# Splitting the second pair's key loads and the first value load in a decode-attention kernel

## The chip, the cores and the metric

The kernel runs on one core of a Trainium2 chip. The metric is the time of one execution on the device in microseconds (us). Engines are called as in the profile: PE is TensorE's matmul side, PEld its weight loads, DVE VectorE, ACT ScalarE, SP the sync engine, which here issues nearly all DMA loads. A ratio of two kernels is the mean time of one's fast runs over the mean of the other's fast runs in the same rounds, so it isn't quite the ratio of the medians that are quoted beside it.

## The reference

One decode step: attention of 16 query heads over a cache of 8192 positions (8 key/value heads of width 256, batch 4), with a small MLP as a gate.

```python
x = A_x                                   # [4, 1, 448] bf16
xn = layernorm(x)
q = (xn @ wq) -> [B, 16, 1, 256]
k, v = repeat(k_cache, 2), repeat(v_cache, 2)   # caches [4, 8, 8192, 256] bf16
p = softmax(einsum("bhqd,bhkd->bhqk", q, k) * 256**-0.5)
s = einsum("bhqk,bhkd->bhqd", p, v) @ wo
return x + s * silu(B(xn))                # B: the gate, on [4, 448] only
```

The two caches are 268 MB, each byte is used once, and all loads together are 279 MB. Everything else is small.

## The kernel before

The 32 key/value heads (8 in each of the 4 batch entries) are worked on in 16 pairs. `kn` holds the keys of one pair (two slots `t` of 4 MiB, 32 KB a partition each), `vb` its values (8 MiB, one buffer). Each of PE's 16 passes transposes the pair's keys through PSUM, makes the scores, and, at the end, multiplies the probabilities of the **pair before** with that pair's values in `vb`. The first pass has no pair before: its value products run on zeros in `pT` and whatever `vb` holds (weights, then), and only afterwards may the first values be loaded into `vb`.

The loads, all from SP, in order:

```python
def load_k(i, t):                       # keys of pair i, slot t
    if i == 0:
        load(kv, src, lo, mid, "dk%d" % t); load(kv, src, mid, hi, "dkh%d" % t)
    elif (i, t) == (1, 1):
        sp.wait_ge(S["v_k"], NVK * (i - 1) + 2)     # first half of slot 1 is free
        load(kv, src, lo, mid, "dk%d" % t)
        sp.wait_ge(S["v_k"], NVK * i)               # second half too
        load(kv, src, mid, hi, "dkh%d" % t)
    else:
        sp.wait_ge(S["v_k"], NVK * (i - 1) + (1, NVK)[t])
        load(kv, src, lo, hi, "dk%d" % t)           # 4 MiB, 32 KB a partition
        ...
def load_v(i):                          # values of pair i
    if i < NPAIR - 1:
        sp.wait_ge(S["v_v"], i + 1)
        load(vv, src, 0, NC2, "dv")                 # 8 MiB, 64 KB a partition
    ...
load_k(0, 0); load_k(0, 1)
load_wo(NLATE, HQ, "dwo")               # early part of the output weights, 2.2 MB
for i in range(1, NPAIR):
    load_k(i, 0); load_k(i, 1); load_v(i - 1)
```

The end of a pass on PE. `PV_PARTS` says how many of the 128 pieces of values are done between which of the last scores:

```python
PV_PARTS = (0, 8, 16, 28, 72, NC2)
for i, f in enumerate(tail):            # last three scores, then two steps of the row maximum
    if t == NS - 1:
        f_pv(vv, PV_PARTS[i], PV_PARTS[i + 1], NC2)   # signals p_pv after the last one
    f()
f_sum()
```

And on DVE, where `v_v` is what releases `vb` to the next load:

```python
f_negb()                                # waits for PE's step after the last value product
f_rz()
take(v, "p_pv")
v.sem_inc(S["v_v"], 1)
v.sem_inc(S["v_pt"], 1)
f_po()
```

## Time and profile before

| | before |
|---|---|
| median time | 656.48 us (655.72 to 656.78, 3 runs) |
| profiled run | 657.7 us, span 656.4 us |
| bytes loaded | 279 MB |
| PE busy / ACT busy / DVE busy | 77% / 40% / 39% |

The first view is the page of the profiled run of the kernel before: its span, then three rows in 40 equal slices of 16.4 us each. PEclk is PE's granted clock in tenths (9 is 90% or more), DMA the busy share of the 16 DMA engines in tenths, GB/s what they moved.

```profile
span 656.4 us, 21990 instructions
...
PEclk9997999899796979969697796969989697998967
DMA  9998999999999999999999999999999999999997
GB/s 378 433 429 348 383 445 449 415 423 439 433 461 413 417 447 447 447 401 429 445 446 417 431 433 433 457 415 419 445 425 467 409 425 445 445 417 425 439 426 297
...
```

DMA is busy in every slice. The fourth and fifth slices (49 to 82 us) with 348 and 383 GB/s stand out. A packet counts in the slice in which it begins, so with packets of up to 64 KB single slices scatter about the true rate, up to 467 GB/s here. Spread over each packet's own duration (worked out from the packed trace, since no view prints it), the rate between 100 and 600 us is 433.7 GB/s; 433.6 is used from here on.

The DMA view of the same kernel: all packets, then for two kinds of load the count, the size of one where it is known, and the median us from issue to landing.

```profile
DMA packets 10641, 279.13 MB, mean 425 GB/s; under 512 B 1028, under 2 KB 3080, under 8 KB 3592
...
kn<-in_A_k_cache_dram SPq DMA_DIRECT2D x29, 4096.0 KB, 26.5
...
vb<-in_A_v_cache_dram SPq DMA_DIRECT2D x15, 29.9
```

A load of 4 MiB takes 9.7 us at 433.6 GB/s, yet a typical one lands 26.5 us after its issue: it stands in a queue behind others. With that backlog an earlier issue in later pairs should buy nothing. PE, in turn, waits for the loads.

So the time of this kernel is: bytes over 433.6 GB/s (643.7 us), plus what follows the last landing (2.9 us), plus every stretch in which the DMA engines run dry: 2.6 us in the first 40 us, 5.3 us between 40 and 72 us, and 1.9 us between 600 us and the last landing. The sum is 656.4 us, the span. Here are the stretches of the first pass, from the view by windows. The columns are the window, its length, the busy us and the number of instructions of each engine, the granted clock, the DMA's busy share, and GB/s:

```profile
core 0: us, PE busy (x) PEld busy (x) DVE busy (x) ACT busy (x) POOL busy (x), PEclk, DMA share, GB/s
52.00:56.00 4.00, 1.89 (x46) 1.72 (x43) 0.82 (x2) 1.39 (x2) 0.00 (x0) 1.00 0.91 377
56.00:60.00 4.00, 4.00 (x69) 2.15 (x70) 1.34 (x2) 0.65 (x1) 0.00 (x0) 0.62 0.93 360
60.00:64.00 4.00, 4.00 (x39) 1.11 (x35) 1.44 (x5) 0.00 (x0) 0.00 (x0) 0.52 0.86 348
64.00:68.00 4.00, 3.38 (x56) 2.51 (x48) 2.00 (x5) 1.61 (x8) 0.00 (x0) 1.00 0.87 295
68.00:72.00 4.00, 3.45 (x83) 3.33 (x83) 1.61 (x3) 3.54 (x6) 0.00 (x0) 1.00 0.60 262
```

Here the DMA falls behind for 20 us. These are most of the 5.3 us of loading that are lost between 40 and 72 us. SP's timeline of the same kernel shows the issues (start us, us to issue):

```profile
38.52 0.33 SPq L252 DMA_DIRECT2D kn<-in_A_k_cache_dram  x1
50.12 0.33 SPq L252 DMA_DIRECT2D kn<-in_A_k_cache_dram  x1
57.02 0.33 SPq L252 DMA_DIRECT2D kn<-in_A_k_cache_dram  x1
66.19 0.33 SPq L252 DMA_DIRECT2D vb<-in_A_v_cache_dram  x1
```

These are the first loads of the second pair's keys for slot 0 (4 MiB) and slot 1 (2 MiB at 50.12, 2 MiB at 57.02), and the first values. The last keys land at 66.1 us, the values are issued at 66.19: nothing is queued in between. What the values waited for stands in DVE's timeline; the releasing instruction is between L524 and L528:

```profile
...
65.41 0.16 DVE L520 COPY negb<-psm 128x4 f32<-128x4 f32 x1 [1.83 <-DVEq L307]
65.72 0.18 DVE L524 RECIPROCAL rz<-psw 128x4 f32<-128x4 f32 x1 [0.15 <-DVEq L307]
66.35 0.69 DVE L528 COPY po<-psv 128x512 f32<-128x512 f32 x1 [0.44 <-DVEq L307]
...
```

PE is late in this pass for a reason of its own. Its timeline has these three idle times that nothing in the profile explains ("issue"; the bracket is the idle time before the row):

```profile
36.94 0.24 PE L650 MATMUL psc<-qc,kT 128*128 128x4 bf16 x4 [0.65 <-issue]
...
46.54 0.35 PE L650 MATMUL psc<-qc,kT 128*128 128x4 bf16 x8 [3.81 <-issue]
...
55.11 0.40 PE L637 MATMUL pst<-ident_b,kn 128*128 128x128 bf16 x4 [2.11 <-issue]
```

They lie exactly 124 matmuls apart. With the weight loads, waits and branches between them these are 256 or 257 recorded PE instructions. The DMA records of the packed trace (again in no view) show a fetch of 16 KB of instructions that was done 1.4 us before each gap ended (packets from 34.6, 44.2 and 52.8 us, 0.92 to 0.97 us each). That PE waited for these fetches is the author's reading; the trace shows only the order in time. A boundary (also "block boundary") is one of these places among PE's instructions, passed when PE does the matmul at which the gap ended here. A fetch's delay is counted from the boundary before: the one at 52.8 us began 6.2 us after PE passed the boundary at 46.5.

### The profile page before, as it was taken

The numbers are of one execution on the slowest core, as the hardware profiler recorded it, in microseconds if no ns is written. First come the engines' busy times: TensorE is split into PE (matmuls) and PEld (weight loads), VectorE is DVE, ScalarE is ACT, GpSimd is POOL, SyncE is SP. The second block draws the span as 40 slices with busy tenths as digits, with TensorE's granted clock in tenths as the row PEclk, the third lists the DMA queues.
The fourth block names the chain that finished last, engine by engine and source line by source line (L and its number), as shares of the span: only waits on it lengthen the run. The fifth ranks groups of instructions, "written<-read, shape, count | busy, mean of one in ns | idle before, by whom it ended". The sixth has DMA issues, their size and how long they took to land. (4 is left out here: it accounts for less than half of the span.)

```text
span 656.4 us, 21990 instructions
## 1 busy us (share of the span) xinstructions
PE 502.7 (77%) x9693; PEld 408.6 (62%) x9693; DVE 257.1 (39%) x507; ACT 263.1 (40%) x360; POOL 3.7 (1%) x18
## 2 busy tenths in 40 slices
PE   2878979686895958679594986958589595867957
PEld 0765869476492947649284583938558293765914
DVE  7433545343351524425252352524335152433511
ACT  3432645254260625426063361615436062543601
POOL 2000000000000000000000000000000000000000
PEclk9997999899796979969697796969989697998967
DMA  9998999999999999999999999999999999999997
GB/s 378 433 429 348 383 445 449 415 423 439 433 461 413 417 447 447 447 401 429 445 446 417 431 433 433 457 415 419 445 425 467 409 425 445 445 417 425 439 426 297
DMA packets 10641, 279.13 MB, mean 425 GB/s; under 512 B 1028, under 2 KB 3080, under 8 KB 3592
## 3 DMA queue, kind: packets, MB, share of 16 engines
q1 hardware_dynamic: 10616, 278.99, 98.9%
q8 instruction: 7, 0.11, 0.1%
q14 instruction: 2, 0.02, 0.0%
q10 hardware_dynamic: 16, 0.01, 0.0%
HBM read 278.99 MB, written 0.00 MB: 425 GB/s over the span
## 5 line engine op out<-in xcount | busy, mean ns | idle before, releaser
L637 PE MATMUL pst<-ident_b,kn 128*128 128x128 bf16 x4096 | 300.4, 221 | 23.7 <-PEq L307 21.6
L341 ACT ACTIVATE kT<-pst 128x1024 bf16<-128x1024 bf16 x224 | 226.0, 1023 | 114.1 <-ACTq L307 113.9
L339 DVE COPY kT<-pst 128x1024 bf16<-128x1024 bf16 x288 | 197.5, 691 | 173.7 <-DVEq L307 173.6
L637 PEld LDWEIGHTS pst<-ident_b,kn 128*128 128x128 bf16 x4096 | 238.1, 98 | 25.4 <-issue 25.4
L650 PE MATMUL psc<-qc,kT 128*128 128x4 bf16 x4096 | 174.1, 165 | 11.6 <-PEq L307 6.7
L682 PE MATMUL psv<-vb,pT 128*8 128x512 bf16 x1024 | 106.4, 515 | 98.8 <-PEq L307 98.8
L650 PEld LDWEIGHTS psc<-qc,kT 128*128 128x128 bf16 x4096 | 153.2, 97 | 41.5 <-issue 40.7
L364 ACT ACTIVATE pT<-psc,negb 64x128 bf16<-64x128 f32 x64 | 28.4, 535 | 247.7 <-ACTq L307 247.4
L682 PEld LDWEIGHTS psv<-vb,pT 128*8 128x8 bf16 x1024 | 25.3, 96 | 133.5 <-issue 124.3
L499 DVE TENSOR_REDUCE rmax<-psc 64x2 f32<-64x256 f32 x32 | 13.5, 422 | 137.6 <-DVEq L307 137.4
L675 PE MATMUL psm<-sel,po 128*128 128x4 f32 x136 | 19.2, 264 | 1.6 <-PEq L307 1.6
L675 PEld LDWEIGHTS psm<-sel,po 128*128 128x128 f32 x136 | 18.1, 204 | 1.7 <-issue 1.7
L364 ACT ACTIVATION_READ_ACCUMULATOR pT<-psc,negb 64x1 f32 x64 | 16.4, 256 | 0.0
L528 DVE COPY po<-psv 128x512 f32<-128x512 f32 x17 | 11.7, 691 | 11.5 <-DVEq L307 11.5
L509 DVE TENSOR_REDUCE gmax<-psm 2x2 f32<-2x128 f32 x16 | 4.5, 279 | 26.8 <-DVEq L307 26.8
L520 DVE COPY negb<-psm 128x4 f32<-128x4 f32 x16 | 2.6, 162 | 25.7 <-DVEq L307 25.7
L663 PEld LDWEIGHTS psm<-diag,ones_f 2*128 2x128 f32 x32 | 4.7, 182 | 7.0 <-issue 7.0
L659 PEld LDWEIGHTS psm<-ident_f,rmax 128*2 128x2 f32 x16 | 1.3, 81 | 12.0 <-issue 12.0
L582 PE MATMUL pst<-ident_b,xn_b 4*128 4x4 bf16 x14 | 0.7, 163 | 10.0 <-DVE xn_b L411 10.0
L582 PEld LDWEIGHTS pst<-ident_b,xn_b 4*128 4x128 bf16 x14 | 0.5, 100 | 10.9 <-issue 9.7
L667 PE MATMUL psw<-rowsum,ones_f 128*128 128x4 f32 x34 | 6.7, 269 | 0.0
L663 PE MATMUL psm<-diag,ones_f 2*128 2x4 f32 x32 | 6.1, 258 | 0.0
(93 smaller groups left out, 84.5 us busy)
## 6 DMA issues: line engine op xcount, KB each, us to landing
kn<-in_A_k_cache_dram SPq DMA_DIRECT2D x29, 4096.0 KB, 26.5
kn<-in_A_k_cache_dram SPq DMA_DIRECT2D x6, 2048.0 KB, 24.3
kn<-in_A_v_cache_dram SPq DMA_DIRECT2D x1, 4096.0 KB, 27.7
vb<-in_A_wq_dram SPq DMA_DIRECT2D x1, 3584.0 KB, 11.4
vb<-in_B_w_dram SPq DMA_DIRECT2D x2, 1568.0 KB, 15.7
wo_sb<-in_A_wo_dram SPq DMA_DIRECT2D x1, 2240.0 KB, 40.4
kn<-in_A_v_cache_dram SPq DMA_DIRECT2D x1, 2048.0 KB, 26.2
kn<-in_A_v_cache_dram SPq DMA_DIRECT2D x1, 1280.0 KB, 24.7
```

The source lines that it names most:

```text
L339: engine.tensor_copy(dst, src).then_inc(S["v_ev"], 1)
L341: engine.activation(dst, src, ACT.Copy).then_inc(S["a_ev"], 1)
L364: ins = act.activation(pT[own, 0:NC2 * NR].rearrange("p (c n) -> p n c", n=NR)[:, n], psc[own, 0:NC2 * NR].rearrange("p (c n) -> p n c", n ...
L499: ins = v.tensor_reduce(rmax[own, :], psc[own, 0:NC2 * NR].rearrange("p (c n) -> p n c", n=NR)[:, t * REP:(t + 1) * REP], AX.X, ALU.max)
L509: v.tensor_reduce(gmax[:, :], psm[0:REP, 0:P].rearrange("p (s k) -> p s k", s=NS), AX.X, ALU.max).then_inc(S["v_s"], 1)
L528: v.tensor_copy(po[:, :], psv[:, 0:CP * DH]).then_inc(S["v_po"], 1)
L637: ins = pe.transpose(dst[:, n * P:(n + 1) * P], kn[:, t, GC * j + kl, half * P:(half + 1) * P], ident_b[:, :])
L650: ins = pe.matmul(psc[:, kk * NR:(kk + 1) * NR], kT[:, j % RING, n * P:(n + 1) * P], qc[:, :, half, :], start=(half == 0), stop=(half == N ...
L663: pe.matmul(psm[:, P:P + NR], ones_f[0:REP, :], diag[:, :], start=True, stop=True).then_inc(S["p_m2"], 1)
L667: pe.matmul(psw[:, 0:NR], ones_f[:, :], rowsum[:, :], start=True, stop=True).then_inc(S["p_s"], 1)
L675: ins = pe.matmul(psm[:, o:o + NR], po[:, i * DH + dh:(i + 1) * DH:NHALF], sel[:, i, 0:NR], start=(i == 0), stop=(i == CP - 1))
L682: ins = pe.matmul(psv[o:o + CP * NR, 0:CP * DH], pT[:, kk * NR:(kk + CP) * NR], src[:, kk:kk + CP, :].rearrange("p c d -> p (c d)"), start ...
```

## The change

Its intent: let the DMA run on where it runs dry, by (1) loading the second pair's keys in pieces of 8 KB a partition, (2) loading the first values in two halves, each released when PE's value products have passed it, and (3) releasing `vb` on DVE before two small operations. The boundary 72 of the value products moves to 64, so that a half ends on it.

```diff
+    NKP = 4
-    PV_PARTS = (0, 8, 16, 28, 72, NC2)
+    PV_PARTS = (0, 8, 16, 28, NCH, NC2)          # NCH = 64
 ...                                              # load_k
+                sp.wait_ge(S["v_k"], NVK * (i - 1) + 1 + t)
+                if i == 1:
+                    for n in range(NKP):
+                        if t == 1 and n == NKP // 2:
+                            sp.wait_ge(S["v_k"], NVK * i)
+                        load(kv, src, lo + n * NCH // NKP, lo + (n + 1) * NCH // NKP, "dk%d" % t)
 ...                                              # load_v
-                if i < NPAIR - 1:
+                if i == 0:
+                    sp.wait_ge(S["p_vh"], 1)
+                    load(vv, src, 0, NCH, "dv")
+                    sp.wait_ge(S["v_v"], 1)
+                    load(vv, src, NCH, NC2, "dv")
+                elif i < NPAIR - 1:
                     sp.wait_ge(S["v_v"], i + 1)
                     load(vv, src, 0, NC2, "dv")
 ...                                              # DVE, end of a pass
+                take(v, "p_pv")
+                v.sem_inc(S["v_v"], 1)
                 f_negb()
                 f_rz()
-                take(v, "p_pv")
-                v.sem_inc(S["v_v"], 1)
                 v.sem_inc(S["v_pt"], 1)
 ...                                              # PE, end of a pass
-                            f_pv(vv, PV_PARTS[i], PV_PARTS[i + 1], NC2)
+                            ins = f_pv(vv, PV_PARTS[i], PV_PARTS[i + 1], NC2)
+                            if PV_PARTS[i + 1] == NCH:
+                                ins.then_inc(S["p_vh"], 1)
+                            if PV_PARTS[i + 1] == NC2:
+                                ins.then_inc(S["p_pv"], 1)
```

The rest of the diff only makes the semaphore counts agree (a slot of keys now counts 64, a pair's values 32) and signals the last pair's products from the place where `f_pv` is called. No arithmetic is added.

More of the change, by code (lines that the diff above doesn't have):

```diff
@@ L198, in bass_recurrent_scan__gqa_block_cached__mixer_s_mlp__decode_kernel @@
         S = {n: es.enter_context(nc.semaphore(n)) for n in (
-            ["dx", "dwq", "dw3", "dw4", "dwo", "dk0", "dk1", "dkh0", "dkh1", "dv", "dout", "pause"]
+            ["dx", "dwq", "dw3", "dw4", "dwo", "dk0", "dk1", "dkh0", "dkh1", "dv", "p_vh", "dout", "pause"]
             + ["dvl%d" % i for i in range(NPIECE)] + ["dwl%d" % i for i in range(len(LATE))]
@@ L261, in load_k @@
                     load(kv, src, mid, hi, "dkh%d" % t)
-                elif (i, t) == (1, 1):
-                    sp.wait_ge(S["v_k"], NVK * (i - 1) + 2)
-                    load(kv, src, lo, mid, "dk%d" % t)
-                    sp.wait_ge(S["v_k"], NVK * i)
-                    load(kv, src, mid, hi, "dkh%d" % t)
-                else:
-                    sp.wait_ge(S["v_k"], NVK * (i - 1) + (1, NVK)[t])
+                    sp.sem_inc(S["dk%d" % t], 16 * (NKP - 1))
+                    return
+                sp.wait_ge(S["v_k"], NVK * (i - 1) + 1 + t)
[4 more added lines that the diff above has]
+                        load(kv, src, lo + n * NCH // NKP, lo + (n + 1) * NCH // NKP, "dk%d" % t)
+                else:
+                    if t == 1:
+                        sp.wait_ge(S["v_k"], NVK * i)
                     load(kv, src, lo, hi, "dk%d" % t)
-                    if t == 1:
-                        sp.sem_inc(S["dkh1"], 16)
+                    sp.sem_inc(S["dk%d" % t], 16 * (NKP - 1))
             def load_v(i):
                 src = pair(A_v_cache, i)
-                if i < NPAIR - 1:
+                if i == 0:
[4 more added lines that the diff above has]
+                elif i < NPAIR - 1:
                     sp.wait_ge(S["v_v"], i + 1)
                     load(vv, src, 0, NC2, "dv")
+                    sp.sem_inc(S["dv"], 16)
                 else:
@@ L449, in prog_dve @@
             v.sem_inc(S["v_po"], 1)
-            v.sem_inc(S["dv"], 16)
+            v.sem_inc(S["dv"], 32)
             v.wait_ge(S["g_c"], NPC)
@@ L627, in f_t @@
                 if j == 0:
-                    take(pe, "dk%d" % t, 16)
+                    take(pe, "dk%d" % t, 16 * NKP)
                 if j == NGR // 2:
-                    if t == 0:
-                        pe.wait_ge(S["dkh0"], 16)
-                    else:
-                        take(pe, "dkh1", 16)
+                    pe.wait_ge(S["dkh%d" % t], 16)
                 dst = pst[j % NST][:].bitcast(BF16)
@@ L685, in f_pv @@
                                     start=(kk < NCG * CP), stop=(kk >= end - NCG * CP))
-                if hi == end:
-                    ins.then_inc(S["p_pv"], 1)
+                return ins
             def body():
@@ L699, in body @@
                         tail += [f_rmaxT, f_bc]
-                        take(pe, "dv", 16)
+                        take(pe, "dv", 32)
                     for i, f in enumerate(tail):
                         if t == NS - 1:
-                            f_pv(vv, PV_PARTS[i], PV_PARTS[i + 1], NC2)
+                            ins = f_pv(vv, PV_PARTS[i], PV_PARTS[i + 1], NC2)
[3 more added lines that the diff above has]
+                                ins.then_inc(S["p_pv"], 1)
                         f()
@@ L750, in finish @@
                     take(pe, "dvl%d" % i, 16)
-                    f_pv(kv, PIECES[i], PIECES[i + 1], pb)
+                    ins = f_pv(kv, PIECES[i], PIECES[i + 1], pb)
+                ins.then_inc(S["p_pv"], 1)
                 take(pe, "v_a")
```

## The prediction

> **What bounds the kernel now.** The DMA. Its packets in the trace, spread over their own durations, give 433 to 434 GB/s in almost every 2 us from 72 to 648 us. [...] 279 MB at 434 GB/s are 643 us; the span is 656.4. PE is busy 77% (page), and from 95 us on its timeline has a gap of 3 to 8 us in every pair, until keys land. A 4 MiB key load takes 9.7 us; in later pairs loads are issued 19 to 31 us before they land: a backlog stands, and an earlier issue there is worth nothing.
>
> The one hole lies between 52 and 72 us. In 2 us steps from 56 us the rate is 407, 300, 388, 372, 87, 115, 334, 411 GB/s. Against 434 the hole is worth 5.0 us (3.6 of them from 64 on). In SyncE's timeline the second half of the second pair's second keys is issued at 57.0 and lands at 66.1; the first values (8 MiB) are issued only at 66.2, when the value products of the first pass and VectorE's small work after them have ended; the first packet starts at 67.15.
>
> The first pass is late on PE for another reason: its timeline has gaps of 0.65, 3.81 and 2.11 us (ending at 36.9, 46.5, 55.1), each about 1.4 us after a 16 KB instruction fetch (packets at 34.6, 44.2, 52.8) was done. Later passes lack both. I read them as fetches held up behind data packets.
>
> **What the change does.**
> 1. The first half of the first values needs only the products up to piece 64, which end near 62.0. Its issue moves from 66.2 to about 62, its first packet to 63, before the keys ahead of it have landed. This closes most of the hole from 64 us on: 3.3 us.
> 2. The second half is released before VectorE's two small operations: under 1 us earlier, hidden behind the 9.7 us of the first half. In other pairs the backlog hides it: 0.
> 3. The second pair's keys come in packets of 8 KB, not 32 and 16. A fetch behind them should wait less: the 2.11 us gap shrinks to under 1 us; the 3.81 us gap has the output-weight load ahead of it and mostly stays. PE reaches its marks some 1.5 us earlier, the keys' second half is issued near 55.5, the dip at 58 us shrinks: 0.9 us. Cost: perhaps 1% lower rate (16 KB took 611 ns, 32 KB 1213), 0.2 us; more issues of 0.33 us on an idle queue, nothing.
>
> All of this is on the critical path: every byte not moved in the hole moves the end. What follows the last landing (2.9 us) stays. Sum: 3.3 + 0.9 - 0.2 = 4.0, up to 4.5 us.
>
> **Predicted: 652.2 us, 8 in 10 between 650.6 and 654.2.** Faster by over 2%: 0.01; within 2%: 0.98; slower: 0.01.
>
> **What would show it.** Slices 4 and 5 of the page's GB/s row (348, 383) above 410; the first values issued at 60 to 62.5 us; later key loads landing 4 to 5 us earlier; PE's waits for keys in later pairs as long as before; the gap near 55 us shorter, that near 46 us not.
>
> **What would make it wrong.** Fetches wait for something other than packet length (then 653.3); DMA ramps slowly after restarts; the backlog of pairs 2 and 3 proves too thin and the hole moves there.

## More of the kernel before

In the view of the waits, this is the largest one on PE (total us, times, longest us); it stands before the value products:

```profile
PE psv L682 <- PEq L307: 98.8, 14, 8.3
...
```

These are waits for values: those of one pair landed at 126.71 us and their products began at 126.85, the next at 165.38 and 165.52, and so on.

## The result, and the profile after

The changed kernel took 653.0 us in the median (652.77 to 653.14, 4 runs) against 656.62 us (655.72 to 656.78, 4 runs) of the kernel before. The ratio of the fast runs is 0.9947, with a 95% interval of 0.9930 to 0.9965. That is within 2%, by the forecast's classes, and 3.6 us in size.

The same rows of the page, for the changed kernel:

```profile
span 651.4 us, 22024 instructions
...
PEclk9989999797896979889697997969889797987968
DMA  9999999999999999999999999999999999999997
GB/s 378 435 413 434 441 423 465 404 457 412 456 425 425 453 412 449 421 437 439 431 440 425 441 447 404 457 412 457 412 445 439 421 453 412 453 414 441 437 416 308
...
```

The two low slices now read 434 and 441. By windows (same columns as before):

```profile
core 0: us, PE busy (x) PEld busy (x) DVE busy (x) ACT busy (x) POOL busy (x), PEclk, DMA share, GB/s
52.00:56.00 4.00, 3.77 (x82) 2.83 (x81) 1.34 (x2) 1.02 (x1) 0.00 (x0) 1.00 1.01 428
56.00:60.00 4.00, 3.31 (x55) 1.17 (x52) 1.44 (x5) 0.00 (x0) 0.00 (x0) 1.00 1.02 424
60.00:64.00 4.00, 3.11 (x53) 2.59 (x46) 2.23 (x5) 2.30 (x9) 0.00 (x0) 1.00 1.08 459
64.00:68.00 4.00, 3.91 (x89) 3.77 (x86) 1.84 (x3) 3.46 (x4) 0.00 (x0) 1.00 1.09 469
68.00:72.00 4.00, 4.00 (x93) 4.00 (x93) 1.69 (x4) 2.36 (x3) 0.00 (x0) 1.00 0.97 418
```

None is below 418 GB/s. Spread over durations, 0.65 us are lost between 40 and 72 us, in place of 5.3. SP's timeline: second pair's keys for slot 0 and slot 1 (first of each group of loads), then both halves of the first values.

```profile
39.10 0.33 SPq L253 DMA_DIRECT2D kn<-in_A_k_cache_dram  x1
48.23 0.33 SPq L253 DMA_DIRECT2D kn<-in_A_k_cache_dram  x1
54.12 0.33 SPq L253 DMA_DIRECT2D kn<-in_A_k_cache_dram  x1
57.32 0.33 SPq L253 DMA_DIRECT2D vb<-in_A_v_cache_dram  x1
60.61 0.33 SPq L253 DMA_DIRECT2D vb<-in_A_v_cache_dram  x1
```

The values are issued at 57.32 and 60.61 us while the keys ahead of them go on landing until 64.8. And PE's gaps in its first pass:

```profile
37.52 0.24 PE L657 MATMUL psc<-qc,kT 128*128 128x4 bf16 x4 [1.74 <-issue]
...
45.90 0.35 PE L657 MATMUL psc<-qc,kT 128*128 128x4 bf16 x8 [1.02 <-issue]
...
52.23 0.38 PE L644 MATMUL pst<-ident_b,kn 128*128 128x128 bf16 x4 [1.21 <-issue]
```

Two of the three are shorter, one is longer. PE reaches its first value product at 54.0 us, in place of 56.9. Its largest wait in later pairs is about as long as before, as forecast:

```profile
PE psv L689 <- PEq L317: 101.6, 16, 7.3
...
```

In later pairs keys and values land 3.9 to 4.9 us earlier than before.

The span in the profiles fell by 5.0 us, but the median of the times by 3.6. The profiled run of the kernel before, at 657.7 us, was one of its slower runs.

### The profile page after: what moved, and what is told of

Its sections match the earlier page's. It is cut to its first block, busy times and chain, and to the rows that moved or that the text cites. A ratio compares the mean times of both kernels' runs of the same rounds, so it can differ in the third digit from the quotient of the medians.

```text
span 651.4 us, 22024 instructions
## 1 busy us (share of the span) xinstructions
PE 495.4 (76%) x9693; PEld 405.7 (62%) x9693; DVE 257.2 (39%) x507; ACT 263.3 (40%) x360; POOL 3.7 (1%) x18
## 5 line engine op out<-in xcount | busy, mean ns | idle before, releaser
L689 PE MATMUL psv<-vb,pT 128*8 128x512 bf16 x1024 | 101.5, 493 | 100.8 <-PEq L317 100.1
L689 PEld LDWEIGHTS psv<-vb,pT 128*8 128x8 bf16 x1024 | 24.4, 92 | 132.8 <-issue 121.5
L689 PE MATMUL psv<-kn,pT 128*8 128x512 bf16 x58 | 5.1, 505 | 1.6 <-PEq L317 1.6
```

What stands on the lines that cost most here:

```text
L689: ins = pe.matmul(psv[o:o + CP * NR, 0:CP * DH], pT[:, kk * NR:(kk + CP) * NR], src[:, kk:kk + CP, :].rearrange("p c d -> p (c d)"), start ...
```

## The experiments

All gave correct results. There were three sets of rounds on one chip. The first two had 11 runs each of the kernel before, the third added one to the second's; these runs took 654.4 to 659.5 us, with medians of 656.35, 655.44 and, for the second and third together, 655.97. The rows "before" and "after" are the first measurement, told above. The table has for each kernel the times, and from its one profile: when PE began its first value product, when the first values were issued, when the keys ahead of them had landed, the difference of the last two (the lead), and the DMA time lost between 56 and 72 us. "Lost" is the stretch less its bytes over 433.6 GB/s, with each packet spread over its duration. It holds two seams: the values, and just before them the second half of slot 1's keys (issued at 57.0 us in the kernel before, 2.5 us before the load ahead had landed). In the first three rows 1.2, 1.1 and 0.7 us of the loss lie before 64 us, so not all of it belongs to the lead in the same row. Each lead is from one profile and moves with PE's clock, as the first experiment shows.

| kernel | median us (lowest to highest; runs) | value products begin | first values issued | keys ahead land | lead | lost 56-72 |
|---|---|---|---|---|---|---|
| before | 656.48 (655.72 to 656.78; 3) | 56.9 | 66.2 | 66.1 | 0.0 | 4.9 |
| before_again | 656.48 (one run) | 56.8 | 63.3 | 66.3 | 3.0 | 2.2 |
| values_only | 653.47 (652.88 to 654.78; 6) | 55.8 | 61.1 | 64.8 | 3.7 | 1.3 |
| keys_only | 654.08 (653.34 to 655.69; 6) | 55.2 | 61.7 | 65.0 | 3.3 | 0.8 |
| keys_and_order | 652.98 (652.74 to 653.67; 6) | 53.6 | 60.4 | 64.5 | 4.2 | 0.1 |
| halves_together | 653.13 (652.93 to 653.69; 6) | 55.2 | 60.8 | 64.7 | 3.9 | 0.2 |
| old_order | 653.06 (652.90 to 653.12; 4) | 53.6 | 56.9 | 64.7 | 7.8 | 0.2 |
| keys_n2 | 652.83 (652.61 to 652.89; 6) | 55.0 | 60.2 | 64.4 | 4.2 | 0.1 |
| after_again | 652.97 (652.63 to 653.11; 6) | 54.4 | 59.6 | 64.7 | 5.1 | 0.2 |
| after | 653.00 (652.77 to 653.14; 4) | 54.0 | 57.3 | 64.8 | 7.5 | 0.2 |
| keys_n16 | 654.04 (653.97 to 654.16; 4) | 54.4 | 59.3 | 65.6 | 6.3 | 0.6 |
| hold_keys | 659.65 (one run) | 53.2 | 60.9 | 71.7 | 10.8 | 0.1 |
| wo_later | 657.91 (656.37 to 659.29; 4) | 53.8 | 57.1 | 63.9 | 6.8 | 1.5 |

The last three lost their time elsewhere: keys_n16 in the shorter packets themselves, hold_keys 7.1 us between 40 and 56 us, wo_later at earlier seams.

### The kernel before, profiled again (before_again)

No edit.

> A second profile of the kernel before, unchanged, to see how much of the first pass's lateness is the same every time. If instruction fetches are held up systematically, PE again shows gaps of some 6.5 us in sum in its first pass (at 36, 46 and 55 us), the granted clock again falls to half for some 7 us in the value products, and the first values are again issued at 65.5 to 66.5 us. If the fetches are a matter of luck, the gaps' sum differs by over 2 us and the issue by as much. The stretch from 52 to 72 us loses 5 us of DMA time in the first case, 3 or less in the other.

The gaps are there again at the same matmuls (2.29, 1.35 and 1.75 us; 5.4 in sum, against 6.6 in the first profile). But the rest of the pass was faster. In the first profile PE's granted clock was half for 6.8 us, from 57.0 to 63.8, and the value products took 8.0 us; in this one the clock was full there, and they took 5.3. So the first values were issued 2.9 us earlier, and only 2.5 us of loading were lost between 40 and 72 us, where the first profile had lost 5.3. So the gaps came back as expected, the half clock and the late issue did not: the gaps came at the same places, the length of the pass differed. The hole had a different size in the two profiles. It isn't the only thing that varies: this run's time was only 1.2 us below the first's, because 0.5 us more were lost between 120 and 600 us and 1.0 us more between 600 us and the last landing. The times of the kernel before on this chip spread over 5 us; how much of that is the hole was not measured, since only these two runs were profiled.

### One part alone (values_only, keys_only), and the whole again (after_again)

values_only is the changed kernel with the key loads (and their counts) of the kernel before. It keeps the new order on DVE:

```diff
-                if i == 1:
-                    for n in range(NKP): ...      # 8 KB a partition
+                elif (i, t) == (1, 1):            # slot 1 in 16 KB, slot 0 in one load of 32 KB
+                    ...
```

> Values in two halves, released by the products, with the second pair's keys loaded as in the kernel before (32 and 16 KB a partition). Theory A (both parts count: the halves pull the issue forward by about 4 us, the short packets let the fetches through and pull PE forward): PE as late as before, first values issued near 62, the loss after 64 us gone but the 1.2 us between 56 and 64 us stays: 653.4 us. Theory B (only the halves count, PE's early arrival in the changed kernel was luck): 652.8, a little better than the whole change because 32 KB packets carry 1% more. Theory C (only PE's pace counts): 655.5 to 656.5.

653.47 us, 2.9 less than the 656.35 of its rounds (ratio 0.9961, interval 0.9941 to 0.9982). The values were issued at 61.1, 3.7 us before the keys ahead of them had landed, and still 0.6 us were lost after 64 us, and 0.7 before. This is Theory A's number; Theory B's 652.8 is near enough that the next run has to decide. In this profile PE's clock was at half during the value products, from 52.7 to 63.0 us.

keys_only is the kernel before with the new key loads only:

```diff
+    NKP = 4
-                elif (i, t) == (1, 1): ...        # 16 KB a partition
+                if i == 1:
+                    for n in range(NKP): ...      # 8 KB a partition
```

> Second pair's keys in loads of 8 KB a partition, first values in one load and VectorE's order as before. Theory A: PE is 2 to 4 us earlier, first values issued at 61.5 to 63.5 us, while the keys ahead still load until 64.8: 653.0 to 654.0 us. Theory B: PE as late as before, 656.6 + 0.2 = 656.8. Theory C: the same as the whole change, 653.0.

654.08 us, 2.3 less (ratio 0.9973, interval 0.9953 to 0.9994). It is Theory A's band, and Theory B, in which short packets do nothing, is out. Theory C, in which they do everything, asked for the whole change's time and for nothing from values_only; both failed.

> The whole change again, for a second profile and a time on the chip of the two parts. All theories: 653.0 us. Theory A: first values issued at 57 to 59 us, gaps of PE's first pass 5 us or less in sum and no stretch at half clock in the value products, as in the first profile. Theory B: the first profile was luck, and the issue comes near 62 us.

652.97 us, in a band of 0.5 us (652.63 to 653.11), where the kernel before spread from 654.4 to 658.5 in the same rounds. In this profile PE's clock was again at half, from 53.9 to 60.7 us, and the value products took 7.8 us, almost as long as in the slow profile of before. The values came at 59.6 in place of 57.3, and that cost nothing. So the whole change does not only close the mean hole, it puts enough lead before it to absorb PE's uneven pace. The expectation of no half clock was wrong, and the issue was just outside the 57 to 59 us expected; the gaps, 4.3 us in sum, were within it.

The two runs' gains sum to 5.2 us, the whole gives 3.4: each closes much of the same hole.

### Release or size? (halves_together, keys_and_order, old_order)

halves_together is the changed kernel with both halves of the values waiting for the later release:

```diff
-                    sp.wait_ge(S["p_vh"], 1)
+                    sp.wait_ge(S["v_v"], 1)
                     load(vv, src, 0, NCH, "dv")
-                    sp.wait_ge(S["v_v"], 1)
                     load(vv, src, NCH, NC2, "dv")
```

> The changed kernel with both halves of the first values released together, where the second half is released now; all else kept. If the early release of the first half is what adds to the short key packets, this is like the keys alone: first values issued at 61 to 62.5 us, a dip of the DMA rate at 62 to 66 us worth 0.5 to 1 us, 653.6 to 654.2 us, with a spread of over 1 us between runs. If the size of the two loads (32 KB packets in place of 64) is what counts, it equals the whole change: 653.0 and a spread of 0.5 us.

653.13 us, 0.2 more than the whole, with ranges that overlap (652.93 to 653.69 here). So, with short key loads, the early release of the first half is worth next to nothing in the median, and the expectation's reading was that the smaller packets of the values then made the difference to keys_only. But these two also differ in DVE's order, so the reading was tested: keys_and_order is keys_only with the new order, and the values still in one load.

```diff
+                take(v, "p_pv")
+                v.sem_inc(S["v_v"], 1)
                 f_negb()
                 f_rz()
-                take(v, "p_pv")
-                v.sem_inc(S["v_v"], 1)
```

> The keys in 8 KB loads and VectorE's new order, with the first values still in one load of 64 KB a partition. It differs from the run with both halves released together only in that one load. If VectorE's order (release about 0.8 us sooner) made the gain of that run over the keys alone, this takes 653.1 to 653.5 us, with the first values issued near 61 us, 3.7 us or more before the keys ahead of them have landed. If the smaller loads of the values made it, this stays at 653.8 to 654.3, like the keys alone.

652.98 us, the time of the whole change and a little under the range expected: the reading by size is out, DVE's order fits. Its effect is visible in the timelines. In keys_only, DVE and then SP:

```profile
60.94 0.16 DVE L524 COPY negb<-psm 128x4 f32<-128x4 f32 x1 [1.35 <-DVEq L311]
...
```

```profile
61.73 0.33 SPq L253 DMA_DIRECT2D vb<-in_A_v_cache_dram  x1
```

The values are issued 0.8 us **after** this small copy began. In keys_and_order:

```profile
60.63 0.16 DVE L524 COPY negb<-psm 128x4 f32<-128x4 f32 x1 [2.62 <-DVEq L311]
...
```

```profile
60.35 0.33 SPq L253 DMA_DIRECT2D vb<-in_A_v_cache_dram  x1
```

They are issued 0.3 us **before** it. With a lead of 3.3 us keys_only lost 0.8 us between 56 and 72 us, with 4.2 keys_and_order lost 0.1. Not all of the lead need come from the order, since the keys also began 0.7 us earlier in this run, but the traces separate the two: from the end of the last value product (60.48 and 60.17 us) to the issue it took 1.25 us in keys_only and 0.18 in keys_and_order, so the order moves the issue by 1.1 us. For the times, the two kernels ran in different rounds, with ranges that overlap. So 1.1 us is an estimate of what the order is worth there, from the two medians.

old_order is the whole change with DVE's order as it was.

> The whole change with VectorE's old order. The first half of the values is issued by the products' own mark and is 9.7 us of loading; the second half's release 0.8 us later is hidden: 653.0 us, and a spread of 0.5 us or less. A rival in which VectorE's order carries the gain in all sixteen pairs would give 653.5 or more.

653.06 us, within 0.1 of the whole. Where the first half is released early, the later release of the second half is hidden behind it. The order and the early half are two ways to the same lead: one of them is enough in the median.

### Packet size (keys_n2, keys_n16)

The changed kernel with `NKP = 2` (16 KB a partition) and `NKP = 16` (2 KB).

> The changed kernel with the second pair's keys in loads of 16 KB a partition. Rate in those 8 MiB a little higher (16 KB in 611 ns against 2 times 309 or 310): 0.15 us faster if PE's pace is the same, 652.8. If packet length sets the fetches' delay, they take about 5 us and PE reaches the value products about 1 us later; the lead of the first values, 5 us or more, still hides that. If the dips at the seams depend on 8 KB packets, dips come back at 57 us and it is 653.3 or more.

> The changed kernel with the second pair's keys in loads of 2 KB a partition. If a fetch waits for packets in proportion to their length, it now begins under 4 us after the boundary at 46 us, and PE is earlier still; but packets of 1.8 KB moved some 5% slower (the output weights, 408 GB/s), so 8 MiB cost about 1 us more: 653.8 to 654.2 us. If the fetch waits for a number of packets or for something else, its delay is not below the 4.2 us seen with 8 KB.

652.83 and 654.04 us, both as expected in time. Of the rest, the lead in keys_n2 was 4.2 us and not 5 or more, and in keys_n16 the fetch began 4.5 us after the boundary, so the branch in which the delay follows packet length is out. keys_n2 is 0.14 us below the whole change, with ranges that overlap, so no better kernel is claimed. The price of short packets is in the trace: 84 ns for 2 KB, 309 for 8 KB, 611 for 16 KB and 1213 for 32 KB, which are 24.4, 26.5, 26.8 and 27.0 GB/s on one engine.

What the packets do for PE is seen best in when its value products began: at 56.9, 56.8 and 55.8 us in the three profiles with keys of 32 KB in slot 0 (hold_keys, below, in which they were held back, left out), and at 53.6 to 55.2 in the seven with 8 KB (those of the table and wo_later below), 55.0 with 16 KB, 54.4 with 2 KB. The last two lie within the range of the seven, so no difference between 2, 8 and 16 KB is shown. Nor is it shown that shorter gaps make the whole difference: the three gaps sum to 6.6, 5.4 and 4.1 us in the three profiles with 32 KB and to 2.7 to 5.4 in the seven with 8 KB.

### What the instruction fetch waits for (hold_keys)

The kernel before with the first key load of the second pair held until PE is half through slot 1, so that the queue is empty for 4 to 5 us:

```diff
-                    sp.wait_ge(S["v_k"], NVK * (i - 1) + (1, NVK)[t])
+                    sp.wait_ge(S["v_k"], 2 if (i, t) == (1, 0) else NVK * (i - 1) + (1, NVK)[t])
```

> The kernel before, with the second pair's first key load held back until PE is half through the first pass's second keys (near 50 us, in place of 38.5), so that the DMA queue is empty from about 45 to 50 us. It will be slower by about 5 us; what counts is the instruction fetch that follows PE's passing of the block boundary at 46 us. So far the fetch packet began 5.8 to 6.2 us after PE passed the boundary with 32 KB key packets in the queue, 4.2 to 4.5 us with 8 KB packets. Theory F (fetches are held up by queued data): with the queue empty it begins under 2 us after the boundary, and PE's gap near 53 us vanishes. Rival G (a fetch takes 4 to 6 us whatever the queue holds): it begins 5 us or more after it, and the gap of about 2 us stays.

659.65 us (one run), slower as it must be. With no data queued, the fetch began 3.05 us after PE passed the boundary, in place of 5.8 to 6.2 with 32 KB packets and 4.2 to 4.5 with 8 KB, and the gap at the next boundary was gone. So Rival G is out: at this boundary, and in one profile, the fetch came sooner with the queue empty. That queued data hold fetches up fits this, and fits the order of the three groups. Theory F's "under 2 us" failed too: some 3 us are there without any data. Nor is it a matter of packet length alone, since 2 KB packets (4.5 us) were no better than 8 KB.

### The early weights moved away (wo_later)

```diff
-            load_wo(NLATE, HQ, "dwo")
             for i in range(1, NPAIR):
                 load_k(i, 0)
                 load_k(i, 1)
                 load_v(i - 1)
+                if i == 1:
+                    load_wo(NLATE, HQ, "dwo")
```

> The whole change with the early part of the output weights (2.2 MB, 5.3 us of loading) moved from ahead of the second pair's keys to behind the first values. Lead theory (the rate holds only if a load is issued 4 us or more before the one ahead has landed): the second pair's keys are then issued near 39 us while the load ahead of them lands near 39.6, a lead of half a microsecond, and a hole of some 3 us opens at 38 to 44 us; later seams keep leads of 2 to 4 us and lose up to 1 us: 655.5 to 657 us. If only the gap at the first values had mattered, 653.0. Also: the instruction fetch after the block boundary at 37 us began 6.1 to 7.3 us later in all runs, with these weights in the queue; if they hold it up, it now begins 5 us or less after the boundary, and the PE gap near 45 us shrinks.

657.91 us (656.37 to 659.29, 4 runs), slower than expected. By windows of 2 us:

```profile
36.00:38.00 2.00, 1.10 (x27) 1.10 (x27) 0.24 (x1) 0.77 (x1) 0.00 (x0) 1.00 0.67 287
38.00:40.00 2.00, 1.69 (x48) 1.61 (x46) 1.09 (x2) 0.00 (x0) 0.00 (x0) 1.00 0.27 70
40.00:42.00 2.00, 2.00 (x47) 2.00 (x44) 1.38 (x2) 1.38 (x2) 0.00 (x0) 1.00 0.96 377
...
50.00:52.00 2.00, 0.52 (x15) 0.40 (x12) 0.69 (x1) 0.59 (x1) 0.00 (x0) 1.00 0.80 229
52.00:54.00 2.00, 2.00 (x48) 1.86 (x47) 0.82 (x2) 1.02 (x1) 0.00 (x0) 1.00 0.98 381
54.00:56.00 2.00, 2.00 (x42) 1.09 (x42) 0.52 (x1) 0.00 (x0) 0.00 (x0) 1.00 1.03 430
56.00:58.00 2.00, 2.00 (x35) 0.76 (x31) 1.42 (x5) 0.00 (x0) 0.00 (x0) 1.00 1.06 295
58.00:60.00 2.00, 1.31 (x24) 0.28 (x12) 0.03 (x1) 0.00 (x0) 0.00 (x0) 1.00 0.93 287
60.00:62.00 2.00, 2.00 (x29) 1.85 (x29) 0.95 (x3) 0.57 (x3) 0.00 (x0) 1.00 1.10 434
```

The 4 us of the expectation's theory fit rows of the table measured before it (0.8 us lost with a lead of 3.3 us in keys_only, 0.1 with 4.2 in keys_n2). The first hole, at 36 to 40 us, is the one expected: the second pair's keys could be issued only at 38.5, with almost nothing queued ahead. So the 5.3 us of weights had bridged the time in which PE had not yet freed a key slot. The later dips were a surprise in size. The loads at 47.7 and 53.9 us had leads of 4.2 and 3.5 us, and the rate still fell to 229 and 287 GB/s in these windows. A lead of 4.2 us was enough in keys_and_order and keys_n2, and was not here.

The second half of the expectation failed outright. The fetch after the boundary at 37 us still began 6.1 us after it, and the gap that followed was 2.7 us, with the weights gone and the queue almost empty at 38 to 40 us. So it does not take the weights to hold that fetch. The queue was not empty for long, though: the last keys of the first pair landed at 39.4 us, and from 40 us on the second pair's keys filled it again, 3 us before the fetch began. What holds that fetch is open.

## Why the prediction was right or wrong

The measured 653.0 us lies in the range of 650.6 to 654.2, and the change of 3.6 us is near the 4.3 forecast. The prediction's main mechanism, a hole that the change fills, holds. That the sum came out so near is in part luck: the hole bounded it from above, the halves' term was too large (3.3, against 2.9 measured) and the keys' too small (0.7, against 2.3 alone), and parts that were added overlap. By steps:

1. **"What bounds the kernel now. The DMA."** Right. The loss between 40 and 72 us fell from 5.3 to 0.65 us in the first two profiles, that is by 4.65; the last load landed at 648.6 us in place of 653.5, 4.9 earlier, and between 72 and 600 us neither kernel lost anything in these profiles. What follows the last landing is 2.9 us in both. One reading was wrong without harm: PE's gaps of "3 to 8 us in every pair, until keys land" end, from 126 us on, when the values of the pair before land (126.71 us, products from 126.85). Gaps that end with keys are shorter (1.2 to 3.3 us).
2. **"Against 434 the hole is worth 5.0 us."** Right for that run, mis-sized for the kernel. The profile was of a run of 657.7 us; the second profile lost 2.5 us in place of 5.3. The prediction took the hole from a slow run and subtracted it from a median of faster ones. That 1.2 us step down is more than the 0.8 us too many, so it can account for them; with two profiles this is not shown.
3. **"The first half ... closes most of the hole from 64 us on: 3.3 us."** Without the short key loads, but with DVE's new order, both halves gave 2.9 (values_only), so the mechanism holds and the size is near; what the early half gives without the order and the short keys was not run. In the whole change it is not what closes the hole: with short key loads, both halves released together were only 0.2 us slower.
4. **"The second half is released before VectorE's two small operations: ... 0."** Right in the whole change (old_order, 653.06 against 652.97). It is so only because the halves are there: keys_and_order took the whole change's time with the order alone in their place.
5. **"The second pair's keys come in packets of 8 KB ... 0.9 us", less 0.2.** Mis-sized when alone: 2.3 us (keys_only). On top of the halves it is 0.5 (653.47 to 652.97, with ranges that overlap). PE reached its value products about 2 us earlier in place of 1.5 (means of 56.5 and 54.3 us in three and seven profiles). The sum of separate terms was the wrong form: three parts act on one lead.
6. **"The 3.81 us gap has the output-weight load ahead of it and mostly stays."** Wrong as a rule. With the weights in place it was 1.35 us in the second profile of before, about 1 us in both of the whole change, and 2.7 us in five other profiles with keys of 8 or 2 KB; moving the weights away left it at 2.7 us. The other gap, forecast to shrink from 2.11 to under 1 us, was 1.21 and 1.48 us in the two profiles of the whole change and absent in those five.
7. **"The first values issued at 60 to 62.5 us."** 57.3 and 59.6. Between these two profiles the issue moved by 2.3 us: the value products began 0.4 us later, and their first half took 2.0 us longer with the clock at half. The prediction didn't consider this. In the traces the stretches at half clock last 3.4, 6.8 or 10.2 us (once 13.7), and the value products of the first pass met one in before, values_only, keys_n2 and after_again and none in the others. What brings them on is not shown: in the 3.4 us before the clock fell, PE was busy for 55% of the time in before, 57% in after_again and 17% in values_only.

What stays open: what triggers an instruction fetch and what, besides the data queue, delays it; what halves PE's clock, and when; and why a lead of 4.2 us sufficed in two kernels and not in wo_later. (The 16 parts of one load did not land together: they came 1.8 us apart in the whole change, second half of the first values, 82.3 to 84.1 us, and 2.4 us apart in the kernel before, second half of slot 1's keys, 63.7 to 66.1 us.)

## What to carry to other kernels

In a kernel bound by loads, look for the places where little is queued, and ask of each load not whether it is issued before the one ahead has landed, but by how much: here leads of 0 to 3.9 us at the first values went with losses of 4.9 to 0.2 us (in part from the seam before), and 4.2 or more with 0.1 to 0.2, except with 2 KB packets (0.6) and in wo_later, where the dip came at the seam before. This is what these profiles showed at one place, not a threshold. Several small ways to get that lead do not add up, since one hole can be closed only once; the spare ones seem to pay in steadiness (a range of 0.5 us over 6 runs, in place of 4 to 5 over 11). And before sizing a hole from one profile, compare that run's own time with the median, and profile a second time.
